# ConvNeXt-V2 block on one core: eight blocks kept in SBUF instead of six, 33 instead of 35 stored to HBM, and tiles of used blocks and of the convolution serving as load targets and activation buffers

## The chip, the core and the metric

One core of a Trainium2 chip. TensorE (PE), VectorE (DVE), ScalarE (ACT) and GpSimd (POOL) work from their own instruction queues; SP and POOL issue the transfers between HBM and SBUF. The metric is the device time of one execution in microseconds (us), the median of several executions.

## The reference

The input is one image of 512 x 512 pixels with 96 channels in bf16. The reference computes

```
out = depthwise 3x3 convolution of x            (96 channels)
h   = layernorm(out) over the channels
h   = gelu(h @ w1)                              (96 -> 384)
gx  = sqrt(sum over all pixels of h*h + 1e-6)   (one number for each of the 384)
nx  = gx / (mean of gx + 1e-6)
h   = gamma * (h * nx) + beta + h
out = x + h @ w2                                (384 -> 96)
```

The sum over all pixels stands in the middle. The factor that it gives scales h before the second matrix product, so no output pixel can be written before every pixel has gone through the first gelu. The kernel therefore makes two passes.

## The kernel before, in words

The image is cut into 128 blocks of four rows, 2048 pixels each. The 384 hidden values of a block's pixels make a tile of 128 partitions x 6144 values of bf16, 1536 KB, called g here. A g tile has four quarters of 128 x 1536.

**First pass.** It runs in slots (lines 844 to 987). Slot s loads x for a later block, transposes it on DVE into the tile xT, and convolves block s on PE from xT with the weights Wq. ACT evacuates the result into a tile y_bf (`evac`, line 497). POOL squares and normalizes, SP writes the normalized block to HBM (yn_dram) and reads it back with the channels on the partitions (ynT, a ring of six). Some 14 slots later the block's first matrix product and gelu run (`mlp_units`, or in the last 14 slots, which have no convolution any more, `mlp_tail`). The squares for the big sum are taken from g in two ways. A quarter made with the hidden channels on the partitions ("cm") goes through three `bn_stats` on DVE (`entry`, line 671). A quarter made with the pixels on the partitions ("px") goes through twelve 128x128 matmuls g-transposed times g on PE (`gram_next`, line 770). `cm_quads` says how many quarters of a block are cm. A block that is stored or kept must be all cm, since the second product needs that layout.

**What becomes of g.** HBM takes the g tile of 35 blocks (`is_whole`, line 97; stores on SP in three parts of 512 KB, `store_next`, line 755). Six blocks of the last 14 (114, 116, 118, 120, 122, 125; `HELD`, line 91) stay in SBUF. The other 87 are thrown away and recomputed in the second pass. Four of them (`KEPT`, line 92) still have their ynT in the ring; the others read it from HBM again.

**Buffers.** The pool g has five buffers (line 182). Tiles that were needed only by the convolution, xT and xin, hold throw-away g of odd blocks in the last slots (`overs`, line 274). After slot 138 the conv pools are closed (line 976) and pools of the second pass take their place: gr (three g tiles for recomputed blocks), gh (one g tile for block 125), xr (five tiles of x for the residual), gl (two g tiles, targets of the loads of stored g), o (six output tiles).

**Between the passes.** The statistics are gathered into ssq, inverse roots are taken by Newton steps and W2s, the scaled second matrix, is made (lines 990 to 1033). Meanwhile PE and ACT recompute the first six quarters of the second pass (`advance`).

**Second pass** (lines 1045 to 1057). It goes through the blocks in `ORDER`: recomputed blocks in their sequence, and after every second one, roughly, a "free" block that needs no recomputation, either kept or stored. For each block `stage_mm2` (line 326) does 4 sub-steps. One sub-step is twelve matmuls g x W2s into one PSUM bank, one DVE add of the bias row, and, every other one, a DVE add of x over twice the width. `pace` (line 372) puts recomputed quarters evenly between the sub-steps. Each quarter is three 512-column matmuls on PE and one gelu on ACT. At position n, POOL is given the load of x for position n+4 (`load_xr`), and SP or POOL the load for position n+5 (`load_rest`, line 289): SP three reads of ynT for a recomputed block, POOL one load of 1536 KB for a stored block, nothing for a kept one. SP also writes the result of the block before. Every queue takes its work in the order in which it was written down.

Of the kernel before, what the change touches and what calls it, by code (L numbers as in the profile page):

```python
# [12 lines left out]
GR = 4  # L13
# [4 lines left out]
BATCH = 4  # L18
NHELD = 6
WHOLE = (0, 3, 7)  # L20
# [36 lines left out]
def kernel(  # L57
# [32 lines left out]
    TAIL0 = NBLK - NTAIL  # L90
    HELD = [NBLK - 6 - 2 * i for i in range(NHELD - 1)][::-1] + [NBLK - 3]
    KEPT = [NBLK - 5, NBLK - 4, NBLK - 2, NBLK - 1]

    def is_held(q):
        return q in HELD

    def is_whole(q):
        return q < TAIL0 and q % 10 in WHOLE

# [39 lines left out]
    rowsel = consts.tile([128, GR], bf16, name="rowsel")  # L139
    w1_raw = consts.tile([C, E], bf16, name="w1_raw")  # L140
    w1p = consts.tile([128, E], bf16, name="w1p")
    w1s = consts.tile([128, E], bf16, name="w1s")
    Wq = consts.tile([128, NI, 3, GR, 32], bf16, name="Wq")
    w2_sb = consts.tile([128, NCH, C], bf16, name="w2_sb")
# [21 lines left out]
    B2c = consts.tile([128, C], f32, name="B2c")  # L166
    free = [[q for q in range(NBLK) if is_whole(q)], list(HELD)]
    free = [v for i, q in enumerate(free[0]) for v in (free[1][i:i + 1] + [q])]
    made_q = KEPT + [q for q in range(NBLK) if not is_whole(q) and not is_held(q) and q not in KEPT]
    ORDER = []  # L170
    for i, q in enumerate(made_q):
        ORDER.append(q)
        while len(ORDER) - i - 1 < (i + 1) * len(free) // len(made_q):
            ORDER.append(free[len(ORDER) - i - 1])
    assert sorted(ORDER) == list(range(NBLK))
    nth_made = {q: n for n, q in enumerate(made_q)}
    SLOTS = [q % NYT for q in KEPT + [NBLK - 6, NBLK - 3]]

# [6 lines left out]
    p2 = ExitStack()  # L185
    SL = PXP + 2
    with ExitStack() as p1:
# [23 lines left out]
        Y3 = PS[:, 4:7, :]  # L211
        pc = p1.enter_context(ExitStack())
        xinpool = pc.enter_context(tc.tile_pool(name="xin", side="right", bufs=1))
        xin_all = xinpool.tile([128, 4, SL, C], bf16, name="xin")
        xins = {}
# [25 lines left out]
        dwx = g_setup[:9, NI * 9 * 32:NI * 9 * 32 + NI * GR * 32].rearrange("p (i q c) -> p i q c", i=NI, q=GR)  # L241
        zrow = consts.tile([128, W], bf16, name="zrow")
        dve.memset(zrow[:], 0.0)
# [14 lines left out]

        cen = consts.tile([C, 128], bf16, name="cen")
        xtpool = pc.enter_context(tc.tile_pool(name="xt", side="right", bufs=1))  # L260
        ypool = pc.enter_context(tc.tile_pool(name="ybf", side="right", bufs=13))
# [4 lines left out]
        ynpool = pc.enter_context(tc.tile_pool(name="yn", side="right", bufs=3))  # L266
        NXT = 5
        xt_ring = []
        xt_all = xtpool.tile([128, NXT, NI, SL * MB], bf16, name="xT")
        for i in range(NXT):  # L270
            xt_ring.append(xt_all[:, i])
        assert NXT * NI * SL * MB >= NQ * NCH * QW
        assert 4 * SL * C >= NQ * NCH * QW
        overs = [v.rearrange("p a b c -> p (a b c)")[:, :NQ * NCH * QW].rearrange("p (t j w) -> p t j w", t=NQ, j=NCH)
                 for v in (xt_all[:], xin_all[:])]
# [13 lines left out]
        def load_rest(n, sq, pq):  # L289
            q = ORDER[n]  # L290
            v = grp.setdefault(q, {})
            if is_held(q):
                v["g"] = gs[q]
            elif is_whole(q):
                v["g"] = late.gl.tile([128, NQ, NCH, QW], bf16, name="gl")
                pq.dma_start(out=v["g"][:].rearrange("p t j w -> p (t j w)"), in_=g_dram[whole.index(q)])
            else:
                ynt = yn_ring[SLOTS[nth_made[q] % NYT]]
                if q not in KEPT:
                    read_spread(sq, ynt, q)  # L300
                v["ynt"], v["w1"] = ynt, w1p if q in KEPT else w1s

        def recompute(q, t):
            if t == 0:
                grp[q]["g"] = late.gr.tile([128, NQ, NCH, QW], bf16, name="gr")
            cm_unit(grp[q]["g"], grp[q]["ynt"], t, grp[q]["w1"])

        def cm_unit(g, ynt, t, w1=w1p):
            U = banks3()
            for j in range(NCH):  # L310
                pe.matmul(quad_out(U[:, j, :]), lhsT=w1[:, j * 128:(j + 1) * 128],
                          rhs=quad(ynt[:], t), start=True, stop=True)
            act.activation(out=g[:, t, :, :], in_=U, func=ACTF.Gelu_apprx_tanh)

        def px_unit(g, ynt, t):
            Uf = banks3().rearrange("p k w -> p (k w)")
            for r in range(GR):
                c = r * E
                while c < (r + 1) * E:
                    sz = min((r + 1) * E - c, W - c % W)  # L320
                    pe.matmul(Uf[:, c:c + sz], lhsT=ynt[:, r, t * 128:t * 128 + 128],
                              rhs=w1p[:, c - r * E:c - r * E + sz], start=True, stop=True)
                    c += sz
            act.activation(out=g[:, t, :, :].rearrange("p j w -> p (j w)"), in_=Uf, func=ACTF.Gelu_apprx_tanh)

# [32 lines left out]
        XPRE = 4  # L358
        LEAD = 6
        todo = [(n, t) for n in range(NBLK) if ORDER[n] in nth_made for t in range(NQ)]  # L360
        total = len(todo)
# [306 lines left out]
        def flat(b):  # L668
            return gs[b].rearrange("p t j w -> p (t j w)")

        def entry(b, j, m):
            k, e = divmod(ents[b] + m, 32)
            if k not in bsts:
                bsts[k] = bstpool.tile([128, NCH, 32, 6], f32, name="bst")
            dve.bn_stats(out=bsts[k][:, j, e, :], in_=gs[b][:, m, j, :])

        def mlp_tail(b, get):
            if b == HELD[-1]:
                gs[b] = late.gh.tile([128, NQ, NCH, QW], bf16, name="gh")[:]
            elif is_held(b) or b < HELD[0]:  # L680
                gs[b] = gpool.tile([128, NQ, NCH, QW], bf16, name="g")[:]
            elif b > HELD[-1]:
                gs[b] = late.gr.tile([128, NQ, NCH, QW], bf16, name="gr")[:]
            else:
                overs.append(overs.pop(0))
                gs[b] = overs[0]
            for t in range(NQ):
                cm = t < cm_quads(b)
                (cm_unit if cm else px_unit)(gs[b], ynts[b], t)
                gram_next(2 if len(grams) > 4 else 1)  # L690
                if cm:
                    for j in range(NCH):
                        entry(b, j, t)
                if t == 1:
                    for k in get("turn"):
                        stage_turn(k)
                if t == 2:
                    for b2 in get("stats"):
                        stage_stats(b2)
                if t > cm_quads(b):  # L700
                    grams.extend((b, (t - 1) * QC + k * E) for k in range(0, GR, 2))
            for k in get("moments"):
                stage_moments(k)
            if cm_quads(b) < NQ:
                grams.extend((b, (NQ - 1) * QC + k * E) for k in range(0, GR, 2))
# [64 lines left out]
        def gram_next(n):  # L770
            for b, c0 in grams[:n]:
                for c1 in (c0, c0 + E):
                    for j in range(NCH):
                        v = flat(b)[:, c1 + j * 128:c1 + j * 128 + 128]
                        pe.matmul(gram[:, j, :], lhsT=v, rhs=v, start=False, stop=True, skip_group_check=True)
            del grams[:n]
# [67 lines left out]
        for s in range(last_slot + 1):  # L844
# [130 lines left out]
            if s == last_slot - 3:  # L975
                pc.close()
                late.gr = p2.enter_context(tc.tile_pool(name="gr", side="right", bufs=GRB))
                late.gh = p2.enter_context(tc.tile_pool(name="gh", side="right", bufs=1))
                late.xr = p2.enter_context(tc.tile_pool(name="xr", side="right", bufs=5))
                late.gl = p2.enter_context(tc.tile_pool(name="gld", side="right", bufs=2))  # L980
                late.o = p2.enter_context(tc.tile_pool(name="o", side="right", bufs=6))
# [54 lines left out]
    with p2:  # L1036
# [6 lines left out]
        held = None  # L1043
        FIRST = 8
        for n, q in enumerate(ORDER):
            sq, pq = (sp, pool) if n < FIRST else (nc.sync, nc.gpsimd)
            if n + XPRE < NBLK:
                load_xr(n + XPRE, pq)
            if n + PRE < NBLK:
                load_rest(n + PRE, sq, pq)  # L1050
            if n == NBLK - 1:
# [36 lines left out]
```

## Time and profile before

| | us |
|---|---|
| median of 3 runs | 1456.16 |
| the three runs | 1451.85 to 1458.17 |
| profiled execution, its own time | 1458.11 |
| its span, first to last instruction | 1456.3 |
| ACT busy | 1399.4 (96%) |
| PE busy | 1388.1 (95%) |
| DVE busy | 1317.4 (90%) |
| POOL busy | 901.7 (62%) |

The profile comes from one execution, whose time is 1.8 us longer than its span and 2.0 us above the median. The parts of the page are: busy time by engine, the same in 40 slices of the span, the transfer queues, the chain of work that ended last, and the costliest groups of instructions. The trace can also be asked for the busy time in chosen windows, for who waited for whom, and for the instructions in order of time. Nearly every instruction goes through one helper, so it has line 35; groups are told apart by the tiles they read and write. A group line ends with the idle time that its engine spent before it and what ended most of that.

The first pass ends near 952 us. Its last convolution is evacuated at 871 us, and the 14 blocks of the last slots follow, from 875 to 951 us on ACT. The first matmul of the second pass that reads W2s is at 959 us.

### The profile page before, as it was taken

Reading aid. Unit: us, or ns where it says so; the run is one execution under the profiler, and the core shown is the slowest. Engines: PE = TensorE matmul, PEld = TensorE weight load, DVE = VectorE, ACT = ScalarE, POOL = GpSimd, SP = SyncE. Lnnn points to the kernel's source line nnn. Section 1 sums busy time; section 2 is a strip of 40 time slices with the busy share of each in tenths; the row PEclk is TensorE's granted clock in tenths of the full one; section 3 lists DMA queues with packets and bytes.
Section 4 is the critical chain, followed back from the end, with each engine's and each line's share of the span. In section 5 each row is a group of like instructions: output and inputs, shape, how many; then the busy total and the mean of one; then the engine's idle time right before and its main releaser. Section 6 shows DMA issues by size and latency. Waiting matters only on the chain.

```text
span 1456.3 us, 54718 instructions
## 1 busy us (share of the span) xinstructions
PE 1388.1 (95%) x23128; PEld 812.0 (56%) x23128; DVE 1317.4 (90%) x2422; ACT 1399.4 (96%) x1591; POOL 901.7 (62%) x796
## 2 busy tenths in 40 slices
PE   8889999999999999999999998899999999999998
PEld 3444444444444444444444445567777677777776
DVE  7749999999999999999999998778888788888887
ACT  6879999999999999999999999999999899999997
POOL 2559999999999999999899998201111111111110
PEclk9999999999999999999999999999999999999999
DMA  6478889898888988988889876649999999999997
GB/s 195 153 216 234 251 262 278 265 265 260 266 258 270 269 255 269 274 252 267 248 271 274 247 242 204 185 174 371 363 336 368 394 379 415 386 412 413 405 415 307
DMA packets 167275, 421.26 MB, mean 289 GB/s; under 512 B 34198, under 2 KB 83798, under 8 KB 162550
## 3 DMA queue, kind: packets, MB, share of 16 engines
q1 hardware_dynamic: 151508, 313.80, 67.5%
q0 software_dynamic: 14960, 103.82, 18.5%
q8 instruction: 181, 2.97, 0.9%
q14 instruction: 64, 0.52, 0.1%
q10 hardware_dynamic: 562, 0.15, 0.0%
HBM read 261.38 MB, written 156.22 MB: 287 GB/s over the span
## 4 chain that ended last, share of the span: by engine, by line
PE 37%; DVE 36%; ACT 10%; DMA 8%; POOL 4%; issue 3%; SPq 1%; ACTq 0%; POOLq 0%; DVEq 0%
PE PS L35 37%; DVE bst L35 26%; DVE xT L35 7%; ACT g L35 5%; DMA ynT<-yn_dram 3%; DMA yn_dram<-yn 2%; DMA out_dram<-o_sb 2%; ACT y_bf L35 2%; POOL yn L35 2%; ACT gr L35 1%; SPq L35 1%; DVE y_bf L35 1%; POOL ysq L35 1%; DVE o_sb L35 1%; ACT xT L35 1%
## 5 line engine op out<-in xcount | busy, mean ns | idle before, releaser
L35 ACT ACTIVATE g<-PS 128x512 bf16<-128x512 f32 (+2 forms) x1046 | 707.7, 835 | 10.3 <-PE PS L35 6.5
L35 DVE BATCH_NORM_STATS2 bst<-g 128x6 f32<-128x512 bf16 x1086 | 659.0, 672 | 23.5 <-ACT g L35 23.3
L35 ACT ACTIVATE gr<-PS 128x1536 bf16<-128x1536 f32 x356 | 493.1, 1451 | 13.1 <-PE PS L35 8.0
L35 POOL TENSOR_TENSOR yn<-y_bf,rbc 128x1536 bf16<-128x1536 bf16 x126 | 391.3, 3107 | 48.8 <-ACT rbc L35 23.3
L35 PE MATMUL PS<-xT,Wq 64*32 64x511 bf16 (+1 forms) x9198 | 346.1, 389 | 16.8 <-ACT y_bf L35 4.5
L35 PE MATMUL PS<-ynT,w1p 128*128 128x512 bf16 x1170 | 335.4, 382 | 25.4 <-ACT g L35 5.4
L35 DVE TENSOR_TENSOR o_sb<-PS,B2c 128x384 bf16<-128x384 f32 x512 | 280.6, 556 | 70.1 <-PE PS L35 63.6
L35 POOL TENSOR_TENSOR ysq<-y_bf 128x1536 bf16<-128x1536 bf16 x114 | 313.3, 2748 | 26.0 <-ACT y_bf L35 17.8
L35 PE MATMUL PS<-ynT,w1s 128*128 128x512 bf16 x996 | 269.1, 379 | 5.5 <-DMA ynT<-yn_dram 3.3
L285 POOL DMA_DIRECT2D xr<-in_x_dram x116 | 62.2, 537 | 297.9 <-DVE o_sb L35 297.9
L35 PEld LDWEIGHTS <-gr 128*128 128x128 bf16 x4248 | 208.7, 98 | 56.4 <-issue 0.7
L35 PE MATMUL PS<-W2s,gr 128*128 128x96 bf16 x4176 | 218.8, 206 | 0.5 <-DVE o_sb L35 0.4
L35 PEld LDWEIGHTS <-Wq 64*32 64x32 bf16 x9216 | 113.4, 90 | 179.8 <-issue 135.1
L35 ACT ACTIVATE y_bf<-PS 128x1536 bf16<-128x1536 f32 (+2 forms) x135 | 182.4, 1357 | 18.2 <-PE PS L35 18.1
L35 PEld LDWEIGHTS <-w1p 128*128 128x128 bf16 x1170 | 90.4, 98 | 181.1 <-issue 111.5
L35 DVE STREAM_TRANSPOSE xT<-xin 128x576 f32<-128x576 f32 (+1 forms) x256 | 181.5, 748 | 6.5 <-PE PS L35 6.5
L35 DVE TENSOR_TENSOR o_sb<-o_sb,xr 128x768 bf16<-128x768 bf16 x256 | 142.8, 558 | 8.9
L35 PEld LDWEIGHTS <-g 128*128 128x128 bf16 (+1 forms) x1611 | 98.7, 98 | 84.8 <-issue 54.8
L35 PE MATMUL PS<-w1p,ynT 128*128 128x256 bf16 (+2 forms) x828 | 125.8, 272 | 9.7 <-ACT g L35 2.7
L35 PE MATMUL PS<-g 128*128 128x128 bf16 x1368 | 115.3, 221 | 1.2 <-DVE PS L35 1.2
L35 PEld LDWEIGHTS <-w1s 128*128 128x128 bf16 x996 | 79.5, 98 | 46.0 <-issue 5.5
L35 PEld LDWEIGHTS <-gl 128*128 128x128 bf16 x1680 | 82.5, 98 | 23.1 <-issue 0.9
(115 smaller groups left out, 754.9 us busy)
## 6 DMA issues: line engine op xcount, KB each, us to landing
xin<-in_x_dram SPq DMA_DIRECT2D x126, 432.0 KB
g_dram<-g SPq DMA_DIRECT2D x105, 512.0 KB
gl<-g_dram POOLq DMA_DIRECT2D x35, 1536.0 KB, 9.3
yn_dram<-yn SPq DMA_DIRECT2D x512, 96.0 KB
ynT<-yn_dram SPq DMA_DIRECT2D x128, 384.0 KB
out_dram<-o_sb SPq DMA_DIRECT2D x127, 384.0 KB
xr<-in_x_dram POOLq DMA_DIRECT2D x124, 384.0 KB, 7.5
ynT<-yn_dram SPq DMA_DIRECT2D x249, 128.0 KB
```

What stands on the lines that cost most here:

```text
L35: r = f(*a, **k)
L285: pq.dma_start(out=xr[:], in_=x[0, r0:r0 + GR].rearrange("r w c -> (r w) c").rearrange("(p g) c -> p g c", g=PXP))
```

## The change

It has these parts.

- `HELD` has eight blocks: 114, 115, 117, 118, 120, 121, 124, 125. `KEPT` becomes 122, 123, 126, 127. Blocks 110 and 113 are no longer stored; 33 blocks are. 87 are still recomputed.
- With that, `cm_quads` changes: 110 from 4 to 3, 113 from 4 to 2; 115, 117, 121, 124 from 1 to 4; 116 and 122 from 4 to 1.
- In the last slots the g of block 114 lies in xT, that of 116, 119 and then 121 in xin, and that of 122 and 123 in eight y_bf tiles, one for each quarter. 125 keeps gh, 126 and 127 keep gr, the rest the pool g. xT and xin now live to the end of the kernel. Constants that only the convolution reads (w1_raw, Wq, zrow, cen) go to a pool that is closed with the conv pools.
- The pool gl is gone. Stored g is loaded into the g tiles of 114 (in xT) and 115 in turn, once the block that was there has been used. A load whose target is not yet free by the order of the blocks is put off; `user` and `ahead` keep the books.
- `ORDER` spreads the free blocks anew: 114 at position 2 and 115 at 5, the other six kept blocks at 27, 45, 67, 86, 108 and 126, between the stored ones. Before, the six kept blocks stood at 3, 9, 15, 21, 28 and 34, in turn with stored ones, and after 34 every free block was a stored one.

```diff
-    HELD = [NBLK - 6 - 2 * i for i in range(NHELD - 1)][::-1] + [NBLK - 3]
-    KEPT = [NBLK - 5, NBLK - 4, NBLK - 2, NBLK - 1]
+    LASTW = TAIL0 - 4
+    HELD = [TAIL0 + i for i in (0, 1, 3, 4, 6, 7, 10, 11)]
+    KEPT = [NBLK - 6, NBLK - 5, NBLK - 2, NBLK - 1]
+    IN_XT, IN_XIN, IN_GH = TAIL0, TAIL0 + 7, TAIL0 + 11
...
     def is_whole(q):
-        return q < TAIL0 and q % 10 in WHOLE
+        return q < LASTW and q % 10 in WHOLE
...
-    free = [[q for q in range(NBLK) if is_whole(q)], list(HELD)]
-    free = [v for i, q in enumerate(free[0]) for v in (free[1][i:i + 1] + [q])]
+    free, rest = HELD[:2], HELD[2:]
+    for i, q in enumerate(whole):
+        free.append(q)
+        if (i + 1) * len(HELD[2:]) // len(whole) > len(HELD[2:]) - len(rest):
+            free.append(rest.pop(0))
...
-        while len(ORDER) - i - 1 < (i + 1) * len(free) // len(made_q):
+        while len(ORDER) - i - 1 < ((i + 1) * len(free) + len(made_q) // 2) // len(made_q):
             ORDER.append(free[len(ORDER) - i - 1])
...
             elif is_whole(q):
-                v["g"] = late.gl.tile([128, NQ, NCH, QW], bf16, name="gl")
-                pq.dma_start(out=v["g"][:].rearrange("p t j w -> p (t j w)"), in_=g_dram[whole.index(q)])
+                v["g"] = gs[HELD[in_order.index(q) % 2]]
+                pq.dma_start(out=v["g"].rearrange("p t j w -> p (t j w)"), in_=g_dram[whole.index(q)])
...
+        in_order = [q for q in ORDER if is_whole(q)]
+        user = {}
+        for i, q in enumerate(in_order):
+            user[ORDER.index(q)] = ORDER.index(HELD[i] if i < 2 else in_order[i - 2])
...
+        def quarter(b, t):
+            return gs[b][t] if isinstance(gs[b], list) else gs[b][:, t]
...
         def mlp_tail(b, get):
-            if b == HELD[-1]:
+            if b == IN_GH:
                 gs[b] = late.gh.tile([128, NQ, NCH, QW], bf16, name="gh")[:]
-            elif is_held(b) or b < HELD[0]:
+            elif b > IN_GH:
+                gs[b] = late.gr.tile([128, NQ, NCH, QW], bf16, name="gr")[:]
+            elif b == IN_XT:
+                gs[b] = g_xt
+            elif b == IN_XIN or b < IN_XIN and not is_held(b):
+                gs[b] = g_xin
+            elif not is_held(b):
+                gs[b] = []
+            else:
                 gs[b] = gpool.tile([128, NQ, NCH, QW], bf16, name="g")[:]
-            elif b > HELD[-1]:
-                gs[b] = late.gr.tile([128, NQ, NCH, QW], bf16, name="gr")[:]
-            else:
-                overs.append(overs.pop(0))
-                gs[b] = overs[0]
             for t in range(NQ):
                 cm = t < cm_quads(b)
-                (cm_unit if cm else px_unit)(gs[b], ynts[b], t)
+                if isinstance(gs[b], list):
+                    gs[b].append(ypool.tile([128, NCH, QW], bf16, name="y_bf")[:])
+                (cm_unit if cm else px_unit)(quarter(b, t), ynts[b], t)
...
-                late.gl = p2.enter_context(tc.tile_pool(name="gld", side="right", bufs=2))
...
+        ahead = []
         for n, q in enumerate(ORDER):
             sq, pq = (sp, pool) if n < FIRST else (nc.sync, nc.gpsimd)
             if n + XPRE < NBLK:
                 load_xr(n + XPRE, pq)
+            for m in [m for m in ahead if user.get(m, -1) < n]:
+                load_rest(m, sq, pq)
+                ahead.remove(m)
             if n + PRE < NBLK:
-                load_rest(n + PRE, sq, pq)
+                if user.get(n + PRE, -1) < n:
+                    load_rest(n + PRE, sq, pq)
+                else:
+                    ahead.append(n + PRE)
```

## The prediction, made before the changed kernel was run

> **What bounds the kernel now.** I read the busy times first, then the stage table, then the waits inside the stages that the change touches. On the page ACT and PE are both near full, so which of them binds must be read by stage:
>
> ```profile
> PE 1388.1 (95%) x23128; PEld 812.0 (56%) x23128; DVE 1317.4 (90%) x2422; ACT 1399.4 (96%) x1591; POOL 901.7 (62%) x796
> ```
>
> Busy time in windows. The columns are PE, PEld, DVE, ACT, POOL with instruction counts, granted clock, transfer share, GB/s:
>
> ```profile
> 900.00:920.00 20.00, 15.43 (x131) 9.46 (x128) 17.06 (x29) 20.00 (x16) 11.49 (x5) 1.00 0.65 183
> 920.00:940.00 20.00, 16.44 (x148) 10.63 (x146) 14.19 (x24) 20.00 (x16) 3.46 (x2) 1.00 0.64 190
> ...
> 1000.00:1120.00 120.00, 120.00 (x1771) 89.61 (x1770) 102.42 (x190) 118.72 (x87) 19.83 (x37) 1.00 0.98 360
> 1120.00:1240.00 120.00, 115.64 (x1698) 85.97 (x1697) 97.84 (x181) 113.85 (x83) 21.01 (x40) 1.00 1.01 395
> 1240.00:1400.00 160.00, 159.92 (x2362) 119.34 (x2359) 136.75 (x253) 157.90 (x115) 29.91 (x56) 1.00 1.02 406
> ```
>
> The last slots of the first pass are bound by ACT: 20.00 of 20, with PE and DVE below it. The second pass is bound by PE: 120.00 of 120 and 159.92 of 160, except for one stretch, 1120 to 1240, where 4.36 us are missing. What PE waited for in the second pass:
>
> ```profile
> PE PS L35 <- DMA ynT<-yn_dram: 3.3, 4, 2.1
> PE PS L35 <- ACT gr L35: 2.0, 2, 1.1
> PE PS L35 <- DVE o_sb L35: 1.1, 3, 0.4
> ```
>
> So reads of ynT came late, four times, and the chain of work that ended last goes through transfers only there:
>
> ```profile
> 1115.74 9.74 DMA out_dram<-o_sb
> ...
> 1125.50 12.02 DMA ynT<-yn_dram
> ```
>
> To see whether PE time is real, I take two neighbouring groups of the timeline (start, length, operation):
>
> ```profile
> 1196.22 0.81 PE L35 MATMUL PS<-ynT,w1s 128*128 128x512 bf16 x3
> 1196.87 0.67 PE L35 MATMUL PS<-W2s,gr 128*128 128x96 bf16 x12
> 1197.38 0.81 PE L35 MATMUL PS<-ynT,w1s 128*128 128x512 bf16 x3
> ```
>
> Start to start, a recomputed quarter takes 0.65 us and a sub-step 0.51. The window 1240 to 1400 has 343 and 2019 of these matmuls: 114.3 x 0.65 + 168.3 x 0.51 = 160 us, the whole window. A gelu every 1.33 us (951 to 875 us divided by 56 quarters is 1.36) would need only 114.3 x 1.36 = 155 us.
>
> For the seam, DVE in the last slots (the brackets give its idle time before):
>
> ```profile
> 876.52 7.36 DVE L35 BATCH_NORM_STATS2 bst<-g 128x6 f32<-128x512 bf16 x12 [0.48 <-ACT g L35]
> ...
> 936.69 7.22 DVE L35 BATCH_NORM_STATS2 bst<-gh 128x6 f32<-128x512 bf16 x12 [3.50 <-ACT gh L35]
> ...
> 947.48 1.88 DVE L35 BATCH_NORM_STATS2 bst<-gr 128x6 f32<-128x512 bf16 x3 [1.23 <-ACT gr L35]
> ...
> 952.41 0.29 DVE L35 SCALAR_TENSOR_TENSOR junk<-PS,ident_f 128x128 f32<-128x128 f32 x1 [1.04 <-PE PS L35]
> ```
>
> A cm quarter costs DVE about 1.78 us (876.52 to 883.79 holds four, with a start gap). DVE waits for ACT, not ACT for DVE, and just before the statistics are joined it has 1.04 us of slack.
>
> **The change part by part.** The sum is made against the profiled execution, 1458.1 us, 2.0 above the median.
>
> *Stores: six of 512 KB less on SP.* SP issues them at 0.52 to 0.6 us each, 852 to 890 us; no engine waits for g_dram there. Cover: ACT is full. If it were not, SP would still be waiting for its yn_dram writes. 0.
>
> *Squares.* 110 and 113 lose three cm quarters, and the last slots rise from 31 to 37: in all 9 `bn_stats` more and 36 gram matmuls fewer. Twelve gram matmuls take 0.70 us of PE (929.29 to 929.99 in the timeline), so PE sheds 2.1 us, hidden behind ACT. Block 113 with two cm quarters gives a third of the evacuation of block 127 to DVE. ACT then does 128x1024 (mean 1131 ns) instead of 128x1536 (1529): -0.4 us, in a slot led by ACT.
>
> DVE in the last slots: 37 x 1.78 = 66 us in the 76 us of ACT, where 55 were used. The order matters: two kept blocks in a row are 14.2 us on DVE against 10.7 on ACT, and the block after them gives the 3.5 back. I walk it through with DVE starts from the row above. 114 ends at 883.8 as now, 115 at 891.0, the moments of the last batch follow at 891.3 instead of 885.9. POOL's chain of small operations, begun at 887.97, moves by 3.4 us. The turned rstd was at 897.24; two quarters of 117 come before it now, and it lands at 897.3. POOL's next three normalizations slip from 892.6 to 896.0, but SP writes the first of these blocks only at 899.32, when it is done. 117 and 118 end at 908.2, with an aggregate at 909.1; 119 at 910.9; 120 and 121 at 925.2; 122 and 123 at 928.8, where DVE is idle again; 124 at 938.4; 125 at 945.5 instead of 943.9; 127 at 949.8 instead of 949.35. So 0.45 us late against 1.04 of slack: 0. Bounds: 0, and with the second aggregate (0.7 us) and a slower start +1.5.
>
> *New tiles.* 114's first gelu into xT waits for convolutions that precede it on PE anyway. xin is written anew for 119 and 121, three and two blocks after its last use; the last gram of 119 is issued within 120, about 1 us before 121's first gelu. The y_bf tiles of 122 and 123 wait for POOL to have normalized blocks up to 122, near 903 with the slip, against 919. gh now lies over part of the y_bf tile of block 127, normalized by 922.7, against 935.0. All 0; if xin's cover goes, ACT waits under 1.4 us (one gelu).
>
> *Loads into used tiles.* In the changed order every stored block still finds its target used at n-6 at the latest, so each load is still issued five positions ahead; nothing goes into `ahead`. POOL now waits for the same matmuls as with two gl buffers (gl waited 70.1 us in 32 cases, hidden by a five-position lead, 5 x 3.8 = 19 us, against 9.3 to land). Behind it on POOL stand loads of x, as before. Issue time 533 ns as before. 0.
>
> *Second pass, work.* 512 sub-steps and 348 quarters, as before: PE is unchanged. Two loads of 1.573 MB go, of 128 x 2 x 0.393 + 83 x 0.393 + 35 x 1.573 = 188 MB.
>
> *Second pass, spread.* A group of two recomputed blocks and a stored one moves 3 x 0.786 + 2 x 0.393 + 1.573 = 4.72 MB in 12 x 0.51 + 8 x 0.65 = 11.3 us, 417 GB/s. Before, 30 of the 35 loads stand in the last 91 positions; now 33 stand nearly evenly in positions 8 to 123, and the mean is 185 MB over 485 us, 382 GB/s. The 4.36 us were lost at 395 GB/s, none at 360 and 0.1 at 406, so the load alone doesn't fix the loss. Its bounds are 0 (the rows at 360 and 406) and 4.4 again; beyond that see the rivals. 382 lies between two rows without loss and every fifth or sixth load now has a gap behind it: I take 1.0. That is -3.4.
>
> Sum: 1458.1 - 0.4 - 3.4 = 1454.3. Since the runs before spread over 6 us and the profiled one is 2.0 above their median, part of its 4.4 us loss is probably missing in the median run; the same sum from the median gives 1452.3. I take the middle, **1453.4 us**. 0.5% is 7.3 us, about what a measurement of this kernel can tell from no change.
>
> A rule against PE as the bound: the Trainium skill, "SBUF — State Buffer", section "Summary: rules for kernel authors", says to reckon transfers to and from HBM at about 358 GB/s. By an estimate from that page the 188 MB would take 525 us, more than the second pass has, and the bytes saved would count in full. The trace moves 406 GB/s over 160 us here, so that figure doesn't hold for this core.
>
> **Rivals.**
>
> *Transfers bind the second pass.* For it: share 1.00 to 1.02 after 1120, SP waits 102 us for earlier transfers before it issues ynT. Against: PE is full at 406. Gain 3.15 MB / 0.406 = 7.7 us, and 0.4: about 1448. This is the case that the 358 GB/s of the Trainium skill's page "SBUF — State Buffer" would make certain.
>
> *The loss only moves.* The dense loads now start at position 8 rather than 37, so the late ynT reads come near 1000 to 1060 and cost 4.4 again: 1456.
>
> *Loss all along the pass (slower).* SP issues a read only after an older transfer has landed; landing takes 10 to 12 us when busy. If the stretch 1120 to 1240 shows the steady rate of a dense order (3.6%), and only that the rest was lucky, then some 420 us outside the gaps of kept blocks lose 15 us instead of 4.4: 1458.1 + 10.9 - 0.4, less 1 for the median, 1467. It decides once more than 120 us run at that rate. Against: 160 us at 406 without loss.
>
> *DVE's backlog reaches W2s.* More than 1.04 us late delays the first sub-step by the excess, 1 to 3 us: 1455.5.
>
> **How the numbers follow.** Forecast 0.48, loss moves 0.16, backlog 0.08: all within 0.5%, 0.72. Transfers bind: 0.16, faster. Loss all along: 0.12, slower. The range reaches down to take in 1448 less its spread of 2, and up to 1463, half way into the slower case.
>
> **What would show it.** Right: PE's waits for ynT in the second pass fall from 3.3 to about 1; the window 1120 to 1240 fills up; GB/s is near 380 from 1000 on; the last slots keep a gelu every 1.33 us; the `junk` step stays within 1 us of its place after the last gelu. Wrong: ACT below 19.5 of 20 between 880 and 950, waits of POOL or PE for the loads into xT and g, or PE short of its windows near 1000 to 1060.

## The result and the profile after

The changed kernel takes 1461.89 us (median; 1459.41 to 1465.12). The kernel before, run beside it, takes 1453.71 us (1450.91 to 1458.17). The ratio is 1.0056, with a 95% interval of 1.0038 to 1.0074, so it is 8.2 us slower. The forecast was 1453.4 us and no change. The value lies inside the range given, near its upper end, but the direction was given a chance of only 0.12. What brought it there is none of the terms of the sum and none of the rivals as they were written.

The profiled execution of the changed kernel took 1465.12 us, with a span of 1463.3 us. Its page shows the engines as busy as before, in absolute terms. PE has the same 1388.1 us, ACT 0.5 us more, DVE 5.7 us more:

```profile
PE 1388.1 (95%) x23083; PEld 809.0 (55%) x23083; DVE 1323.1 (90%) x2432; ACT 1399.9 (96%) x1591; POOL 900.2 (62%) x794
```

So the time is not in work that was added. The same windows as in the prediction show where it is. The columns are window, length, busy time of PE, PEld, DVE, ACT and POOL with instruction counts, granted clock, transfer share and GB/s:

```profile
900.00:920.00 20.00, 13.87 (x94) 7.34 (x93) 20.00 (x38) 20.00 (x16) 13.08 (x6) 1.00 0.64 180
920.00:940.00 20.00, 15.64 (x134) 9.68 (x132) 16.73 (x29) 19.98 (x16) 3.17 (x2) 1.00 0.71 209
1000.00:1120.00 120.00, 116.31 (x1702) 86.27 (x1700) 98.53 (x182) 114.55 (x84) 21.05 (x40) 1.00 1.00 390
1120.00:1240.00 120.00, 116.34 (x1703) 86.31 (x1701) 98.56 (x183) 114.22 (x83) 19.83 (x37) 1.00 0.99 375
1240.00:1400.00 160.00, 158.14 (x2319) 117.49 (x2318) 134.83 (x249) 155.67 (x113) 28.42 (x54) 1.00 0.99 382
```

ACT stays full in the last slots from 900 us on, as before. PE is short in all three windows of the second pass, by 3.69, 3.66 and 1.86 us. Before, it was short in one, by 4.36. What PE waits for there has kept its name and more than doubled, as the waits of PE from 960 us on say (total, times, longest):

```profile
PE PS L34 <- DMA ynT<-yn_dram: 7.5, 12, 2.3
PE PS L34 <- ACT gr L34: 2.3, 3, 1.0
PE PS L34 <- DVE o_sb L34: 1.1, 3, 0.4
```

The chain of waits that ended last, for the second pass, goes through PE for 63.9% of it (82.3% before) and through transfers for 27% (13% before):

```profile
by line: PE PS L34 63.9%; DMA ynT<-yn_dram 16.2%; DMA out_dram<-o_sb 10.7%; ACT gr L34 3.9%; DVE o_sb L34 3.2%; issue 0.7%; SPq L129 0.6%; ACTq L34 0.0%
```

One link of it, from the chain between 1080 and 1130 us, shows what such a loss is made of. An output write takes 10.20 us and then a ynT read takes 12.12 us. The read is not issued until the write has landed:

```profile
1090.69 10.20 DMA out_dram<-o_sb
...
1100.90 12.12 DMA ynT<-yn_dram
```

One measure sums the second pass up, and I use it for all kernels below: the time from the start of the first matmul that reads W2s to the start of the last one. It is 492.7 us before (959.2 to 1451.9) and 499.1 us after (959.5 to 1458.6). So 6.4 of the 7.0 us between the two profiled executions lie in this stretch, 0.3 in all that comes ahead of it, and 0.3 behind it. PE's idle time between 960 and 1440 us grows by 4.7 us, from 5.58 to 10.26. From the first to the last matmul with W2s it grows by 4.7 us too, from 6.8 to 11.5. The remaining 1.7 us are counted as busy time of PE; the page of the profile says that the ends of matmuls are modelled, and where these 1.7 us come from was not settled.

### The profile page after: what moved, and what is told of

It is laid out like the page before. It is cut to its first block, busy times and chain, and to the rows that moved or that the text cites. A ratio compares the mean times of both kernels' runs of the same rounds, so it can differ in the third digit from the quotient of the medians.

```text
span 1463.3 us, 54619 instructions
## 1 busy us (share of the span) xinstructions
PE 1388.1 (95%) x23083; PEld 809.0 (55%) x23083; DVE 1323.1 (90%) x2432; ACT 1399.9 (96%) x1591; POOL 900.2 (62%) x794
## 2 busy tenths in 40 slices
DMA packets 166123, 414.97 MB, mean 284 GB/s; under 512 B 34070, under 2 KB 83670, under 8 KB 161654
## 4 chain that ended last, share of the span: by engine, by line
PE 34%; DVE 22%; DMA 16%; ACT 15%; POOL 6%; issue 4%; SPq 2%; POOLq 0%; ACTq 0%; DVEq 0%
PE PS L34 34%; DVE bst L34 15%; ACT g L34 8%; DMA ynT<-yn_dram 6%; DVE xT L34 4%; DMA out_dram<-o_sb 4%; DMA yn_dram<-yn 3%; ACT y_bf L34 3%; POOL yn L34 3%; ACT gr L34 2%; SPq L34 2%; DMA rbc<-r_dram 2%; POOL ysq L34 1%; POOL nt L34 1%; DMA xin<-in_x_dram 1%
## 5 line engine op out<-in xcount | busy, mean ns | idle before, releaser
L34 PE MATMUL PS<-ynT,w1p 128*128 128x512 bf16 x1179 | 339.3, 384 | 31.5 <-ACT g L34 6.9
L34 PE MATMUL PS<-ynT,w1s 128*128 128x512 bf16 x996 | 269.2, 379 | 10.2 <-DMA ynT<-yn_dram 7.5
L34 ACT ACTIVATE y_bf<-PS 128x1536 bf16<-128x1536 f32 (+2 forms) x143 | 192.9, 1367 | 14.0 <-PE PS L34 10.3
L34 PEld LDWEIGHTS <-g 128*128 128x128 bf16 (+1 forms) x2415 | 138.0, 98 | 95.5 <-issue 53.5
L34 PE MATMUL PS<-w1p,ynT 128*128 128x384 bf16 (+2 forms) x810 | 123.7, 272 | 7.4 <-ACT xin L34 2.6
L34 PEld LDWEIGHTS <-ynT 128*128 128x128 bf16 x810 | 62.5, 97 | 29.8 <-issue 12.1
```

The costliest lines, as they stand in the source:

```text
L34: r = f(*a, **k)
```

## The experiments

**What could have done it.** The second pass has the same matmuls as before, so the reads of ynT must have become late in another way. Three theories were set against each other.

- *A, the lead.* A recomputed block's read is issued by position: SP issues it five positions before the block's place in `ORDER`. But its use is not tied to that place. `pace` computes recomputed quarters evenly by index, so quarter number k runs at a time that doesn't depend on the order. The new rounding in `ORDER` (`+ len(made_q) // 2`) puts each free block half a step sooner. Then 42 of the 83 blocks that are read stand one position later than before, and their reads are issued one position later, while they are used at the same time. Worked out from the code (from five positions ahead of the block to the sub-step behind which `pace` asks for its first quarter), the mean lead falls from 3.42 positions to 2.91, the least from 3.00 to 2.50. A position lasts 3.8 us here (485 us divided by 128), so 1.9 us of some 13.0 are lost.
- *B, the dense order.* The kept blocks now stand among the stored ones over the whole pass, so loads of stored blocks, ynT reads and output writes are mixed throughout, and this mix loses time at any place. This was the slower rival of the prediction.
- *C, the tiles.* Load targets that were used by kept blocks, fewer buffers, or the new last slots hold something up.

The lead can be read in the traces: from the issue of the last of a block's three reads to the first matmul that uses the block. The mean over the 77 read blocks behind the first six is 11.45 us before and 10.64 us after. Leads under 10 us are 15 before and 28 after.

The landing of a read can be seen too. SP's transfers use eight semaphores in turn. Each landing raises one of them in sixteen updates, and SP issues the next transfer on that semaphore only behind the sixteenth. From the issue of a block's last read to that update it takes 8.32 us on the mean before and 8.29 after. So the reads don't land later in the changed kernel: they are issued later against their use. I call a read late when PE's first matmul of the block starts within 0.15 us of the landing. Late reads are 10 before and 21 after. They are more than the waits listed above, where waits under 0.15 us are left out.

This table holds the numbers of all kernels. The ratio is to the kernel before, with its 95% interval. "Second pass" is the measure above. "Idle" is PE's idle time from 960 to 1440 us. All but the ratio are from one profiled execution each, and these lie from 2.9 us below the median of their kernel's runs (reads later) to 7.7 above it (kernel before with reads earlier). The one of the kernel before is 2.0 above, the changed one's 3.2 above, that of the kernel before with new rounding 1.4 below. So the ratio says what a change costs, and the other columns say how.

| kernel | ratio | second pass, us | PE idle, us | mean lead, us | leads under 10 us | late reads |
|---|---|---|---|---|---|---|
| before | 1 | 492.7 | 5.6 | 11.45 | 15 | 10 |
| changed | 1.0056 [1.0038, 1.0074] | 499.1 | 10.3 | 10.64 | 28 | 21 |
| changed, measured again | 1.0045 [1.0018, 1.0072] | 501.2 | 12.7 | 10.94 | 20 | 19 |
| changed, old rounding | 0.9997 [0.9969, 1.0024] | 494.5 | 6.4 | 12.39 | 6 | 5 |
| before, new rounding | 1.0016 [0.9986, 1.0046] | 492.0 | 4.1 | 10.40 | 31 | 16 |
| before, new spread | 0.9964 [0.9941, 0.9987] | 490.3 | 3.9 | 11.82 | 6 | 5 |
| before, new spread and rounding | 1.0030 [1.0006, 1.0054] | 497.4 | 9.7 | 10.87 | 21 | 14 |
| changed, reads one position earlier | 0.9948 [0.9924, 0.9972] | 485.9 | 0.9 | 14.12 | 1 | 0 |
| the same, measured again | 0.9950 [0.9929, 0.9971] | 485.9 | 0.9 | 14.69 | 0 | 0 |
| changed, old rounding, reads earlier | 0.9957 [0.9940, 0.9973] | 485.8 | 0.2 | 15.79 | 1 | 0 |
| before, reads earlier | 0.9954 [0.9928, 0.9979] | 495.6 | 7.9 | 13.27 | 11 | 14 |
| changed, reads and moments earlier | 0.9941 [0.9918, 0.9964] | 485.9 | 1.2 | 14.20 | 1 | 0 |
| changed, reads one position later | 1.0137 [1.0102, 1.0172] | 512.3 | 21.5 | 8.51 | 63 | 27 |

### The changed kernel with the old rounding

```diff
-        while len(ORDER) - i - 1 < ((i + 1) * len(free) + len(made_q) // 2) // len(made_q):
+        while len(ORDER) - i - 1 < (i + 1) * len(free) // len(made_q):
```

> The changed kernel, but the free blocks are placed by the old rounding down, so that each recomputed block stands at the position in the second pass that it had before. Theory A (late reads): the new rounding puts the recomputed blocks half a position later on the mean, while the recomputation keeps its even pace, so each ynT read has about 0.5 x 3.8 = 1.9 us less before PE needs it; with the old rounding the time returns to that of the kernel before, 1452 to 1455 us (ratio 0.998 to 1.001), and PE's waits in the second pass fall to 2 to 4 us. Rival B (dense loads from position 8 on): nothing is won, ratio 1.004 to 1.007. Rival C (the loads into the tiles of used blocks cost more than those into gl): the same as B, 1.004 to 1.007.

Measured: 1454.32 us (1451.67 to 1464.57), a ratio of 0.9997. The loss is gone with one term of one line, while the new tiles and the dense spread are still there. PE's waits in the second pass are back at four late reads, one of them long:

```profile
PE PS L34 <- DMA ynT<-yn_dram: 6.4, 4, 3.4
PE PS L34 <- DVE o_sb L34: 1.1, 3, 0.4
```

B and C fall as causes that are enough by themselves. A has what it asked for.

### The kernel before with the new rounding

```diff
-        while len(ORDER) - i - 1 < (i + 1) * len(free) // len(made_q):
+        while len(ORDER) - i - 1 < ((i + 1) * len(free) + len(made_q) // 2) // len(made_q):
```

> The kernel before with nothing changed but the rounding of the order: the recomputed blocks stand half a position later on the mean. Six kept blocks, 35 stored ones, loads into gl. Theory A: 5 to 9 us slower than before, ratio 1.0035 to 1.006, with 10 or more waits of PE for ynT reads spread over the second pass. Rivals B and C: within 2 us of before, ratio 0.9985 to 1.0015.

Measured: 1458.41 us, a ratio of 1.0016, with an interval that holds 1. The shape is as expected, ten short waits where there were four, but they sum to little:

```profile
PE PS L35 <- DMA ynT<-yn_dram: 4.0, 10, 0.9
PE PS L35 <- ACT gr L35: 1.5, 3, 0.5
```

The mean lead is 10.40 us, even less than in the changed kernel, and the second pass is not longer (492.0 against 492.7 us). But this profiled execution is 1.4 us below its kernel's median, and that of the kernel before 2.0 above. By medians the rounding costs 2.3 us, and the upper end of its interval, 1.0046, reaches into the 1.0035 to 1.006 that A gave. So A in its plain form was not borne out: the measured ratio is under half of what it forecast. That a short lead alone costs nothing is not shown either. In this execution few reads landed slowly: 11 took over 10 us against 23 in the changed kernel, and none more than 11.1 us.

### The kernel before with the kept blocks spread, without and with the rounding

The six kept blocks of the kernel before go between the stored ones over the whole pass, as in the changed kernel. Stored blocks (35) and their gl tiles stay as they were.

```diff
-    free = [[q for q in range(NBLK) if is_whole(q)], list(HELD)]
-    free = [v for i, q in enumerate(free[0]) for v in (free[1][i:i + 1] + [q])]
+    free, rest = [], list(HELD)
+    ws = [q for q in range(NBLK) if is_whole(q)]
+    for i, q in enumerate(ws):
+        free.append(q)
+        if (i + 1) * len(HELD) // len(ws) > len(HELD) - len(rest):
+            free.append(rest.pop(0))
```

> The kernel before with its six kept blocks spread evenly between the stored ones of the second pass (the first stored block comes first), old rounding, so that only which free block stands where changes: loads are dense from the start with a gap after every sixth. Theory A: no recomputed block moves, so within 3 us of before, ratio 0.998 to 1.002. Rival B: the early dense loads alone bring the loss, ratio 1.003 to 1.006. Rival C: within 2 us of before.

> The kernel before with both changes to the order and no other: the six kept blocks spread evenly and the new rounding. 35 stored blocks, loads into gl, the old last slots. Theory A with interaction (a read that is issued half a position later only comes late where loads are dense, and the spread makes them dense from the start): nearly the whole loss of the changed kernel, ratio 1.003 to 1.007. If the loss needs the new load targets or the kept and stored blocks themselves (rival C): 0.997 to 1.002, the sum of the two order changes alone (-0.0036 + 0.0016).

Measured, the spread alone: 1452.24 us, a ratio of 0.9964, and 3.9 us of ynT waits:

```profile
PE PS L35 <- DMA ynT<-yn_dram: 3.9, 4, 1.5
```

Spread and rounding: 1459.6 us, a ratio of 1.0030, and 6.9 us of ynT waits. PE's waits with both:

```profile
PE PS L35 <- DMA ynT<-yn_dram: 6.9, 6, 2.9
PE PS L35 <- ACT gr L35: 3.1, 3, 1.4
PE PS L35 <- DVE o_sb L35: 1.1, 3, 0.4
```

The spread by itself gains: its interval excludes 1. No theory had forecast a gain of this size. With the rounding on top it loses: its interval excludes 1 as well, and the two intervals don't meet. In this spread the rounding moves the ratio by 0.0066, in the old one by 0.0016. This is with 35 stored blocks, two gl tiles and the old last slots, so the order alone can bring a loss. Rival C gave a ratio of 0.997 to 1.002 for the last kernel. The measured value lies above that, though the lower end of its interval (1.0006) lies within. Whether the new tiles and last slots add the rest, up to 1.0045 to 1.0056, can't be told, since the intervals overlap. The same holds with the old rounding: 0.9964 here and 0.9997 in the changed kernel.

### The changed kernel once more

> The changed kernel once more, unchanged, on the chip of the runs that it is sent with, since times of the kernel before spread over 1448 to 1466 us there. Every theory: 1.003 to 1.008 of before, with 10 or more waits of PE for ynT reads. If it is within 1.002, the loss depends on the chip and nothing else that is measured here explains it.

Measured: 1461.11 us, a ratio of 1.0045. The profiled execution has the same kind of waits:

```profile
PE PS L34 <- DMA ynT<-yn_dram: 10.9, 12, 1.9
PE PS L34 <- ACT gr L34: 2.2, 3, 1.0
```

### Reads one position earlier

If the lead is what is short, a longer one must take the loss away and more: also the late reads that the kernel before has. Only the reads of ynT move, from five positions ahead to six. The loads of stored blocks stay where they were.

```diff
+        def is_read(n):
+            return ORDER[n] in nth_made and ORDER[n] not in KEPT
...
-                for n in range(PRE):
-                    load_rest(n, sp, sp)
+                for n in range(PRE + 1):
+                    if n < PRE or is_read(n):
+                        load_rest(n, sp, sp)
...
-            if n + PRE < NBLK:
+            if n + PRE + 1 < NBLK and is_read(n + PRE + 1):
+                load_rest(n + PRE + 1, sq, pq)
+            if n + PRE < NBLK and not is_read(n + PRE):
```

> The changed kernel with one difference: the ynT reads of a recomputed block are issued one position earlier on SP (six ahead in place of five); loads of stored g and of x stay. Theory A: each read gains 3.8 us, twice what the rounding took, so PE's waits for ynT nearly vanish (under 1.5 us) and the time is 1449 to 1453 us, ratio 0.996 to 1.000. Rival B: the transfers are short of rate, an earlier issue only lengthens their queue, 1457 to 1462, ratio 1.002 to 1.006. Rival C: like B.

> The changed kernel with its reads one position earlier, once more beside the other two: 0.9945 to 0.996 of the kernel before under the lead theory, with no wait of over 0.5 us for ynT. A ratio of 0.999 or more would say that the first measurement of it was chance.

> The changed kernel with the old rounding and with ynT reads issued one position earlier: the lead of every read is 1.5 positions longer than in the changed kernel. Theory A: no waits for ynT are left to remove beyond those that the earlier issue alone removed, so the same as that run, 1447 to 1451 us, ratio 0.993 to 0.997. If slower than that by 2 us or more, an early issue costs something on SP's queue.

> The kernel before, with ynT reads issued one position earlier and nothing else. Theory A: its late reads go too (3 to 7 us), so 1448 to 1452, ratio 0.994 to 0.998, and the whole rest of the change (two blocks fewer stored, new buffers, the spread) is then worth less than 2 us either way against the changed kernel with early reads. If it stays at 1.000, the reads were not what held the kernel before.

Measured: 1449.33 us and, again, 1448.31 us on the changed kernel; 1449.18 us with the old rounding; 1449.97 us on the kernel before. The ratios are 0.9948, 0.9950, 0.9957 and 0.9954. On the changed kernel that is more than A forecast the first time (0.996 to 1.000), and in the changed kernel no wait for ynT is left. Its waits of PE in the second pass:

```profile
PE PS L34 <- DVE o_sb L34: 1.1, 3, 0.4
PE PS L34 <- ACT gr L34: 0.5, 1, 0.5
```

And its windows, to be set beside those of the changed kernel above:

```profile
1000.00:1120.00 120.00, 120.00 (x1770) 89.50 (x1768) 103.09 (x190) 118.78 (x86) 22.04 (x41) 1.00 1.01 400
1120.00:1240.00 120.00, 120.00 (x1780) 89.82 (x1779) 102.44 (x190) 118.66 (x87) 21.52 (x41) 1.00 1.00 387
1240.00:1400.00 160.00, 160.00 (x2354) 119.19 (x2352) 137.03 (x253) 158.20 (x115) 28.64 (x54) 1.00 0.99 389
```

PE is full throughout while the transfers move more per second than before. Every profiled execution of the changed kernel with earlier reads has a second pass of 485.8 or 485.9 us. That is close to PE's own time (1.6 us of waits are left in it). The changed kernel exceeds it by 13.2 us, of which 10.2 are idle time of PE (11.5 less 1.3); the kernel before exceeds it by 6.8, of which 5.5 are. The rest is counted as busy. In the new order the two roundings no longer differ clearly (their intervals overlap).

Two more things follow. With early reads on both sides, the changed kernel (0.9948 and 0.9950) and the kernel before (0.9954) can't be told apart, so what is left of the change, apart from the lead, is worth nothing that can be measured. And the times of one kernel scatter less: twelve runs of the changed kernel spread over 19.5 us (1455.14 to 1474.60), twelve with early reads over 7.5 us and, again, over 8.1. The fastest of the 35 runs of the kernel before beside them, 1448.18 us, is no slower than these.

One row doesn't fit. The profiled execution of the kernel before with early reads, 1457.7 us by its span of 1455.9 and the same 1.8 us around it, is at the upper end of that kernel's times (1446.46 to 1457.68) and still waits:

```profile
PE PS L35 <- DMA ynT<-yn_dram: 7.0, 8, 2.2
```

Its median says that early reads help the old order too. Its profile says that they don't always do so there. Why 11 of its leads are still under 10 us was not followed up.

### Reads one position later

The same edit the other way, on the changed kernel:

```diff
                 for n in range(PRE):
-                    load_rest(n, sp, sp)
+                    if n < PRE - 1 or not is_read(n):
+                        load_rest(n, sp, sp)
...
-            if n + PRE < NBLK:
+            if n + PRE - 1 < NBLK and is_read(n + PRE - 1):
+                load_rest(n + PRE - 1, sq, pq)
+            if n + PRE < NBLK and not is_read(n + PRE):
```

> The changed kernel with the second-pass ynT reads issued one position later (four positions ahead, not five), all else as it is. Lead theory: the mean lead falls from 10.75 us to about 7 us while the transfers take 7 to 12 us, so most of the 82 reads come late, by 1 to 4 us each before the delay stretches the following leads: at least 40 us slower than the kernel before, a ratio of 1.03 or more, all of it as TensorE waiting for ynT. If instead the loss comes from crests of the traffic or from the changed tiles, the issue place matters little: under 10 us, a ratio of 1.004 to 1.011.

Measured: 1477.12 us, a ratio of 1.0137. That is 21.2 us over the kernel before, and some 15 over the changed one. The place of the issue matters, which is against the rival, but the size is about half of what the lead theory gave. PE's waits in the second pass:

```profile
PE PS L34 <- DMA ynT<-yn_dram: 17.0, 18, 2.4
PE PS L34 <- ACT gr L34: 5.5, 5, 1.5
```

The waits of SP say in part why it was less. In the changed kernel, reads (L129) stood on SP until an older transfer had landed:

```profile
SPq L129 <- DMA out_dram<-o_sb: 70.1, 40, 3.8
...
SPq L129 <- DMA ynT<-yn_dram: 18.8, 28, 1.8
```

With the reads one position later, that wait for output writes has shrunk:

```profile
SPq L129 <- DMA out_dram<-o_sb: 8.6, 14, 1.1
```

A later read comes when the older transfers have landed already, so it loses less at its issue. The mean lead fell by 2.1 us (10.64 to 8.51) and not by 3.8. The shorter waits for older transfers are worth 1.0 us for each of the 83 blocks; the other 0.7 were not traced. The reads also landed sooner, 6.67 us after the issue on the mean where it was 8.29. I had taken the position for the whole difference.

### Moments of a kept block earlier

The page after has one new wait in the first pass, at 889 us. The timeline there (start, length, operation; the brackets give the idle time before, and its releaser), first DVE, then ACT, then PE:

```profile
885.44 3.65 DVE L34 BATCH_NORM_STATS2 bst<-g 128x6 f32<-128x512 bf16 x6
889.00 0.28 DVE L34 TENSOR_SCALAR mom<-PS 128x128 f32<-128x128 f32 x1
889.38 0.17 DVE L34 MEMSET PS<- 128x128 f32 x1
...
891.63 1.45 ACT L34 ACTIVATE g<-PS 128x1536 bf16<-128x1536 f32 x1 [1.61 <-issue]
...
889.60 0.66 PE L34 MATMUL PS<-xin 128*128 128x128 bf16 x6 [1.41 <-DVE PS L34]
```

The moments of a batch (`stage_moments`) end with a clearing of the statistics bank on DVE. They now stand behind the 24 `bn_stats` of two kept blocks in a row. The next gram matmuls on PE wait for that clearing, and behind them on PE stands the next quarter of the first product, for which ACT waits 1.6 us (the trace names no releaser for this wait; the order of the three engines' rows says so). Not all of the 1.6 us is the clearing's. In this execution the granted clock was 0.50 from 890 to 893 us, and the quarter that ACT waits for took 1.49 us on PE:

```profile
890.05 1.49 PE L34 MATMUL PS<-ynT,w1p 128*128 128x512 bf16 x3
```

In the second execution of the changed kernel, at clock 1.00 there, such a quarter took 0.81 us and ACT waited 0.81 us. The experiment puts the moments right after the last statistics of the batch, in the kernel with early reads:

```diff
                 if t == 2:
                     for b2 in get("stats"):
                         stage_stats(b2)
+                    for k in get("moments"):
+                        stage_moments(k)
...
-            for k in get("moments"):
-                stage_moments(k)
```

> The changed kernel with its second-pass reads one position earlier, and with the moments of a kept block worked out right after its last statistics instruction, not behind the rest of the slot's work on VectorE. If the 1.41 us that TensorE's gram matmuls waited at 889 us for VectorE's clearing of the statistics bank, and the 1.6 us that ScalarE stood idle behind them, are on the path that sets the end of the first pass: 1 to 2 us less than the kernel with early reads alone, so a ratio of 0.993 to 0.9945 to the kernel before where that one has 0.995. If slack ahead of the statistics of the last blocks takes it up: no difference from the kernel with early reads alone.

Measured: 1447.56 us, a ratio of 0.9941. PE's wait for DVE's clearing, 1.4 us in both executions with early reads alone, is gone from the profile. ACT had waited 0.81 us there in these two, at clock 1.00, so less was to be won than the expectation took from the 1.6. The wait of ACT is gone too, and the first matmul with W2s starts at 955.1 us, where the two executions without the edit had 955.8 and 956.1. That goes the right way and is of the right size, but the interval (0.9918 to 0.9964) holds the kernels without it (0.9948 and 0.9950), and the start of that matmul moves by 4 us between executions of one kernel (959.5 and 955.4 for the changed one). Inconclusive. Of all kernels this one has the lowest median. It is faster than both the kernel before and the changed kernel, as is every kernel with early reads.

*Not tried:* the changed kernel with two load tiles of its own again. They would need 24 KB more of each partition beside the tiles that now live to the end, and whether that fits is not shown. So the new targets were separated from the order only from the other side, by the kernel before with spread and rounding.

## Why the prediction was wrong

**The step that failed is "Second pass, spread",** with the sentence in front of it, "512 sub-steps and 348 quarters, as before: PE is unchanged". It took the late reads as a matter of how much is moved per second, found 382 GB/s between two rows without loss, and booked a gain of 3.4 us. The second pass became 6.4 us longer in place of that. The work on PE was indeed unchanged. But the step asked only how dense the loads stand, and never when a read is issued against when it is used. The diff shows the term that moves it: the added `len(made_q) // 2` shifts half of the recomputed blocks by one position, the issue goes by position, and the use does not. The prediction wrote down the five positions for stored blocks ("each load is still issued five positions ahead") and did not ask the same of the recomputed ones, whose reads are issued five positions ahead but used by index. PE's waits for them rose from 3.3 to 7.5 us, where about 1 was forecast. With the old rounding the loss is gone (0.9997); with the reads one position earlier the time is below that of the kernel before (0.9948).

**A gain of the booked size is there, in another kernel.** The spread alone makes the kernel before faster: 0.9964, or about 5 us, where 3.4 were booked. But not by the booked way, as far as its profile shows: its ynT waits sum to 3.9 us, against 3.3 in the kernel before. So the size is luck, or comes from something that one profiled execution doesn't show. In the change the spread comes together with the rounding, and the sum is a loss.

**"Loss all along the pass"** named the right place and the right sign: PE is short in all three windows. Its premise holds (SP does wait for older transfers, and landings in the chain take 9 to 12 us). It named the wrong cause, and about twice the price (10.9 us more loss, against 6.4 us more of second pass). It reasoned that the dense order loses at a steady rate. The dense order with longer leads loses nothing (120.00 of 120 at 400 GB/s).

**"Transfers bind the second pass"** is refuted as a limit of the rate. The changed kernel moves 6.3 MB less in all (414.97 against 421.26 MB) and is slower, and with earlier reads it moves the same bytes 12 us faster. The windows move 387 to 400 GB/s with PE full. The Trainium skill, "SBUF — State Buffer", section "Summary: rules for kernel authors", reckons with about 358 GB/s to and from HBM; no run here is held to that.

**"The loss only moves"** had the right sign of the danger, since the loss did come near 1000 to 1120 us, where there was none. But it also stayed in the next window.

**The first pass came mostly as written, with one miss.** The first matmul that reads W2s starts at 959.5 us against 959.2, so the seam costs nothing that can be seen, and the DVE step before it has 0.82 us of slack left where 0.6 were reckoned (1.04 less 0.45). "DVE's backlog reaches W2s" did not happen. The turned rstd, forecast for 897.3 us, came at 897.03. POOL's waits for its load targets sum to 67 us (70.1 before), hidden, as said. The miss is the clearing of the statistics bank: I followed the 3.4 us delay of the moments into POOL only, and not into PE, where it cost 1.4 us of waiting. With it came a sign of being wrong that the prediction had named, ACT below 19.5 of 20 between 880 and 950: from 880 to 900 us it has 17.71, against 19.87 before. At full clock, in the second execution of the changed kernel, it has 19.19. The 0.4 us from the shared evacuation can't be separated, since the first pass ends up to 4 us apart in two executions of the same kernel (the later one at a mean granted clock of 0.995, the earlier at 1.000).

**What stays open.** With a mean lead of 10.4 us in the old spread the second pass was no longer than before in the one execution profiled, and with one of 10.6 to 10.9 us in the new spread it was 5 to 9 us longer. So the loss seems to need both the shorter lead and the even spread. Why was not shown. The mean landing is the same (8.26 us in the old spread with the rounding, 8.29 in the changed kernel); what differs is the number of slow ones (11 and 23 over 10 us), and one execution of each can't tell whether the spread makes them or chance did. It is not the rate: the changed kernel loses at 375 to 390 GB/s, less than its sibling moves with no loss. Whether the new load targets add a microsecond or two was not settled either.

## What to carry to other kernels

When an order is changed, write down for each prefetch two places: what its issue is counted from, and what its use is counted from. If the two are different (here a position, and an even pace by index), even a rounding term in the order shifts one against the other, and the lead in microseconds has to be set beside the longest landing in the trace, not beside the mean rate. Where PE waits now and then for a late read, test the lead first by issuing one step earlier, since here that was worth more than all of the change.

## What the runs showed of the hardware

- Transfers that look full were not the bound here. The transfer share is 0.98 to 1.02 in the windows shown from 1000 us on, in kernels in which PE waits and in one in which it doesn't; PE was full at 400 GB/s and short at 375.
- Under this load single transfers on SP's queue take 9 to 12 us in the chain of waits of the kernel before and the changed one (8.98 to 12.12 us). A read that was five positions, or 19 us, ahead by its place in the order had only 11 us between its issue and its use (10.64 to 11.45 us on average), since `pace` runs ahead of the order and SP waits before it issues.
- SP's transfers go through eight semaphores in turn, and in all thirteen traces none of these reads was followed by another transfer on its semaphore before its own sixteen updates (231 reads in each, those behind the first six blocks). So SP stands still when the transfer eight places back is slow (70.1 and 18.8 us of waits before reads in the changed kernel).
- Issuing later gave part of the lead back: SP's wait of the reads for older output writes went from 70.1 to 8.6 us, and a position (3.8 us) of lead given away cost 2.1 us.
- DVE's clearing of 128x128 values in PSUM takes 0.17 us, but because it stood last on DVE it held PE for 1.41 us and, as the order of the rows has it, ACT for 0.81 us where the granted clock was 1.00.
- At a granted clock of 0.50 three 128x512 matmuls took 1.49 us, at 1.00 0.81 us. The idle time of ACT behind them was 1.61 us in the one execution and 0.81 in the other.
